# Expert weights in seven packed pieces: how a routed mixture kernel stores and loads its weight forms

## The chip, the cores and the metric

The kernel runs on one core of one Trainium2 chip. The metric is the device time of one execution in microseconds. Of the kernel before there are three runs with a median of 901.46 us. One further execution was recorded by the hardware profiler, and all views of the profile come from it. Engines: PE is TensorE (its weight loads are shown as PEld), DVE is VectorE, ACT is ScalarE, POOL is GpSimd, SP is SyncE, which here issues nearly all DMAs. L1030 means line 1030 of the kernel before.

## The reference

All data are float32. An attention with polynomial features gives `x` (4352 tokens, 128 features), and a mixture of eight experts works on it; each token goes through every expert, with the weights `P` of a Sinkhorn iteration:

```
q_p, k_p = phi(q), phi(k)                 # products of two sketches of 8 numbers: 64 features
num = q_p @ (k_p^T v);  den = q_p . sum(k_p) + 1e-6
x = (num / den)  as (4 * 1088 tokens, 4 heads * 32)
P = exp(x @ w_gate - max); 8 times: rows to sum 1, columns to sum 1, P *= N / E
for e in range(8):                        # w1[e]: 128 x 1024, w2[e]: 1024 x 128
    out += P[:, e] * (relu(x @ w1[e]) @ w2[e])
```

## The kernel before

**Stages.** Attention and routing come first. PE's spare time in them is filled with experts 0 and 1 on part of the tokens, without `P` (`steps()`, written out by `fill`). While the routing runs, the generator `second_forms()` prepares sums of the second weights in HBM. From about 193 us on `weighted()` does all that is left: tokens from 1344 on for experts 1 to 7, the earlier tokens for experts 2 to 7. Since `P` is positive, it is multiplied into `x` ahead of the first product. All engines of this stage run in the order in which the code is written (`manual_schedule`), SP with its queue of DMAs too: a DMA that waits holds all later DMAs of SP.

**Items and half steps.** `wgroups` lists ten groups of token columns (two blocks of 256 columns each in the first five groups, of 224 in the others), `witems` the 60 pairs of a group and an expert. Every second group goes through its experts backwards, so that two items in a row share an expert where a group ends. An item has two half steps (`todo`, s = 0 and 1), each for half of the 1024 hidden features. In the loop over t the generators `firsts(t)` (first products, relu and sums) and `seconds(t - 1)` (second products of the half step before) take turns, product by product.

**Seven products instead of eight.** Both matrix products are done on two by two blocks with seven products of blocks (Winograd's form of Strassen's method) in place of eight. That needs sums of the weight blocks, the forms, besides the blocks themselves. Of the first weights there are eight pieces in the tile `w1x` [128, 8, 256]: four raw blocks (0 to 3) and four sums (4 to 7, made by `sum_first`, L864, on POOL). `firsts` uses seven of them, in the order 0, 4, 5, 7, 6, 2, 3 (L1102 to L1134); raw block 1 is only an input of the sums. Of the second weights `seconds` uses three of the four raw blocks of the tile `w2` [128, 8, 128] and the four sums in the tile `ws` [128, 4, 4, 64]. The last group (`whole`) takes the plain eight products of the second weights, with raw blocks only.

**Where the forms come from.** In the first group (items 0 to 6) and at item 13 the first weights are loaded raw from the input (L857, four DMAs of 128 KB), summed on POOL, and written to a store in HBM (`store_first`, L872, 1 MB). These items are the set `fresh`. All later items load the finished 1 MB tile (L852). The sums of the second weights are built in HBM by `second_forms`: SP writes one half of a sum (`begin`), POOL adds the other half with accumulating DMAs (`add_first`, `add_second`, `add_third`, L905). An item then loads raw `w2` from the input (L861, 512 KB) and `ws` from the store (L862, 512 KB).

**When the weights are loaded.** All three tiles come from pools with two buffers. In the first half step of item i `prepare(i + 1, False)` (L1275) asks for the next item's first weights, in the second half step `prepare(i + 1, True)` (L1283) for its second weights. An item that shares its expert with the one before takes over its tiles.

**What else goes through SP and POOL.** Each item needs a row of `P` spread over all partitions (`load_weights`, L934, for item i + 3), the product of `x` and `P` on POOL (`weigh`, L942) with two DMAs that swap halves of its partitions (L945, for item i + 2), and differences of blocks of `x` (`sum_x`: L951 on POOL, L953 and L955 on DVE). `gate` (L1047) is a copy of one column on ACT that holds POOL's step back until ACT has come to that place. DVE adds PE's results to copies (L1034) and makes the sums of the hidden blocks (L1080 to L1085). At the end of a group its sums are added up (L1218), turned and stored.

Of the kernel before, what the change touches and what calls it, by code (L numbers as in the profile page):

```python
# [50 lines left out]
def kernel(  # L51
# [791 lines left out]
    def form_tiles():  # L843
        return (late[0].tile([P, 8, FORM], F32, tag="w1x", name="w1x"),
                wpool.tile([P, FO, DM], F32, tag="w2", name="w2"),
                wpool.tile([P, 4, FO // 2, H2], F32, tag="ws", name="ws"))

    def load_first(w, e, stored):


        if stored:
            nc.sync.dma_start(out=w[0], in_=form_stores[e][0])  # L852
            return
        for r in range(2):
            for k in range(2):
                rows = H2 * (r ^ k)
                nc.sync.dma_start(out=w[0][H2 * r:H2 * (r + 1), 2 * k:2 * k + 2],  # L857
                                  in_=moe_w1[e][rows:rows + H2].rearrange("p (i r n) -> p r i n", i=2, r=2)[:, r])

    def load_second(w, e):  # L860
        nc.sync.dma_start(out=w[1], in_=moe_w2[e].rearrange("(fo fi) d -> fi fo d", fi=P))  # L861
        nc.sync.dma_start(out=w[2], in_=form_stores[e][1])  # L862

    def sum_first(i):  # L864
        w1, g = forms[i][0], nc.gpsimd
        g.tensor_tensor(w1[:, 4], w1[:, 1], w1[:, 3], op=Alu.add)
        g.tensor_tensor(w1[:, 5], w1[:, 4], w1[:, 0], op=Alu.subtract)
        g.tensor_tensor(w1[:, 6], w1[:, 0], w1[:, 1], op=Alu.subtract)
        g.tensor_tensor(w1[:, 7], w1[:, 2], w1[:, 5], op=Alu.subtract)

    def store_first(i):
        nc.sync.dma_start(out=form_stores[witems[i][1]][0], in_=forms[i][0])  # L872

    def second_forms():
# [9 lines left out]
        for e in range(1, E):  # L884
            form_stores[e] = (dram.tile([P, 8, FORM], F32, name=f"w1x{e}"),
                              dram.tile([P, 4, FO // 2, H2], F32, name=f"ws{e}"))
# [9 lines left out]
        def begin(e):  # L896
            w, f = rooms[e], form_stores[e][1]
            pin(nc.scalar.mul(w[:, 0], w[:, 0], -1.0))
            pin(nc.sync.dma_start(out=f[:, 0].rearrange("p f d -> p (f d)"), in_=flat(w[:, 1, 0:4])))
            pin(nc.sync.dma_start(out=f[:, 1:3].rearrange("p m f d -> p m (f d)"),  # L900
                                  in_=flat(w[:, 0, 0:4]).unsqueeze(1).to_broadcast([P, 2, FO // 2 * H2])))
            pin(nc.sync.dma_start(out=flat(f[:, 3]), in_=flat(w[:, 0, 4:8])))

        def add(e, out, x):
            pin(nc.gpsimd.dma_start(out=flat(form_stores[e][1][:, out]), in_=flat(x), accum_op=Alu.add))  # L905

        def add_first(e):
            for m in (1, 2):
                add(e, m, rooms[e][:, 1, 0:4])

        def add_second(e):
            for m in (0, 1):
                add(e, m, rooms[e][:, 1, 4:8])

        def add_third(e):
            add(e, 3, form_stores[e][1][:, 1])
# [39 lines left out]

    def same(i):
        return 0 < i < len(witems) and witems[i - 1][1] == witems[i][1]

    def prepare(i, second):  # L960

        if i >= len(witems):
            return
        if same(i):
            forms[i] = forms[i - 1]
            return
        if not second:
            forms[i] = form_tiles()
        if second:
            load_second(forms[i], witems[i][1])  # L970
        else:
            load_first(forms[i], witems[i][1], i not in fresh)
# [24 lines left out]
    def weighted():  # L997
# [16 lines left out]
        def firsts(t):  # L1014
# [10 lines left out]
            def product(out, form, x, start, stop):  # L1025
                for r in range(2):
                    rows = slice(H2 * r, H2 * (r + 1))
                    for col in range(2):
                        o = P * s + H2 * col
                        nc.tensor.matmul(out[H2 * col:H2 * (col + 1), r], w1[rows, form, o:o + H2], xf[rows, x],  # L1030
                                         start=start, stop=stop, tile_position=(H2 * r, H2 * col), skip_group_check=True)

# [375 lines left out]
```

## Time and profile before

| what | value |
| --- | --- |
| three runs | 901.41, 901.46, 903.54 us; median 901.46 |
| the profiled execution | 902.27 us, of which 900.5 from the first to the last instruction (span) |
| mean granted TensorE clock | 0.998 |
| matmuls of the weighted stage | first at 193.0 us, 13489 of them to the end |
| DMA traffic, whole span | 189.90 MB |
| DMA share of the 16 engines, 193 us to the end | 0.69 |

How to read the rows: a group row gives the count of an instruction, its busy time and the mean time of one. A row of waits gives who waited for whom, the us in total, how often, and the longest. "issue" stands for time in which the engine waited for nothing that the profile shows. A windows row gives the stretch in us, its length, the busy time and count of each engine, the granted clock (1.00 is full speed), the share of the 16 DMA engines that was busy (it can come out a little above 1) and GB/s. In the rows of DMA queues q1 is the queue of SP's DMAs and q8 and q14 carry the engines' instructions; a q row gives packets, MB and the share of the engines.

### The profile page before, as it was taken

The page shows a single profiled execution, that of the slowest core. Times are in us where ns is not written, and L with a number is a line of the kernel's source. Part 1 is how long each engine was busy: PE and PEld are TensorE (multiplying, and loading weights), DVE is VectorE, ACT ScalarE, POOL GpSimd, SP SyncE. Part 2 cuts the span into 40 slices and gives each one's busy share as a digit, 9 for nine tenths or more (in the row PEclk, how much of TensorE's full clock was granted, in tenths as well). Part 3 has the DMA queues.
Part 4 walks back from the last instruction along what each step waited for, and adds up shares of the span by engine and source line. Part 5 has one row for each costly group of instructions (what it writes and reads, how often), then busy time and mean ns, then how long its engine had stood idle before and what let it go on. Part 6 is the DMA issues. An engine that isn't in the chain of part 4 may idle for free.

```text
span 900.5 us, 35855 instructions
## 1 busy us (share of the span) xinstructions
PE 888.7 (99%) x15372; PEld 647.6 (72%) x15372; DVE 762.6 (85%) x1325; ACT 546.4 (61%) x1089; POOL 271.0 (30%) x313
## 2 busy tenths in 40 slices
PE   9999999999999998999999999999999999999997
PEld 5777644557667775677777777677897799887896
DVE  7678789888898888888888888888898889889885
ACT  3455476646666664666666666666666666666664
POOL 3121148035551234223213322332232223223220
PEclk9999999999999999999999999999999999999999
DMA  8998599467886873687478658655974984875863
GB/s 240 298 282 243 111 196 201 79 177 230 249 247 189 282 236 110 198 266 230 146 222 246 227 149 241 220 186 153 295 254 106 276 268 132 291 224 187 261 198 90
DMA packets 150686, 189.90 MB, mean 211 GB/s; under 512 B 44512, under 2 KB 122416, under 8 KB 143616
## 3 DMA queue, kind: packets, MB, share of 16 engines
q1 hardware_dynamic: 142784, 177.52, 65.5%
q0 software_dynamic: 6640, 9.95, 5.8%
q8 instruction: 121, 1.98, 0.9%
q14 instruction: 37, 0.30, 0.1%
q10 hardware_dynamic: 1104, 0.15, 0.1%
HBM read 144.97 MB, written 24.16 MB: 188 GB/s over the span
## 4 chain that ended last, share of the span: by engine, by line
PE 95%; DVE 3%; issue 1%; ACT 1%; POOL 0%; DVEq 0%; POOLq 0%
PE pair L1030 38%; PE s L1164 38%; PE a L711 7%; PE s L772 7%; PE a L305 1%; PE a L118 1%; PE a L420 1%; DVE hb L726 1%; PE a L272 0%; DVE hb L1034 0%; PE s L334 0%; PE a L384 0%; DVE hb L1083 0%; PE a L454 0%; PE s L350 0%
## 5 line engine op out<-in xcount | busy, mean ns | idle before, releaser
L1030 PE MATMUL pair<-xf,w1x 64*64 64x256 f32 (+1 forms) x6736 | 513.2, 366 | 1.2 <-DVE hb L1034 1.1
L1030 PEld LDWEIGHTS pair<-xf,w1x 64*64 64x64 f32 x6736 | 269.0, 133 | 87.3 <-DVE hb L1034 7.0
L1034 DVE TENSOR_TENSOR hb<-pair,copies 128x512 f32<-128x512 f32 (+1 forms) x354 | 233.9, 662 | 74.5 <-ACT xf L1047 29.2
L1164 PE MATMUL s<-hb,ws 64*64 64x256 f32 (+1 forms) x3712 | 285.0, 366 | 2.5 <-DVE hb L1084 1.9
L1164 PE MATMUL s<-hb,w 64*64 64x256 f32 (+1 forms) x3040 | 229.6, 364 | 1.2 <-issue 1.2
L1037 ACT ACTIVATE hb<-hb 128x512 f32<-128x512 f32 (+1 forms) x240 | 145.7, 608 | 107.4 <-DVE hb L1034 102.1
L1164 PEld LDWEIGHTS s<-hb,ws 64*64 64x64 f32 x3712 | 153.6, 133 | 47.6 <-DVE hb L1084 2.7
L942 POOL TENSOR_TENSOR xf<-xT,pb 128x512 f32<-128x512 f32 (+1 forms) x60 | 73.4, 1224 | 278.7 <-ACT xf L1047 248.6
L1164 PEld LDWEIGHTS s<-hb,w 64*64 64x64 f32 x3040 | 124.7, 133 | 37.6 <-issue 2.8
L951 POOL TENSOR_TENSOR xf<-xf 128x512 f32<-128x512 f32 (+1 forms) x58 | 70.8, 1222 | 217.7 <-ACT xf L1047 139.0
L711 PE MATMUL a<-xT,w 128*64 128x416 f32 (+3 forms) x512 | 121.2, 466 | 0.0
L1037 ACT ACTIVATE hb<-pair 128x512 f32<-128x512 f32 (+1 forms) x126 | 72.5, 575 | 45.6 <-PE pair L1030 45.6
L713 ACT ACTIVATE hb<-a 128x416 f32<-128x416 f32 (+3 forms) x128 | 59.6, 468 | 65.5 <-PE a L711 53.8
L1080 DVE SCALAR_TENSOR_TENSOR hb<-hb 128x512 f32<-128x512 f32 (+1 forms) x116 | 77.9, 671 | 13.5 <-ACT hb L1037 1.7
L1112 ACT COPY copies<-pair 128x512 f32<-128x512 f32 (+1 forms) x118 | 66.5, 563 | 31.7 <-PE pair L1030 31.7
L1109 ACT COPY copies<-pair 128x512 f32<-128x512 f32 (+1 forms) x118 | 66.5, 563 | 30.7 <-PE pair L1030 30.7
L1103 ACT COPY copies<-pair 128x512 f32<-128x512 f32 (+1 forms) x118 | 66.6, 565 | 27.5 <-PE pair L1030 27.5
L1084 DVE SCALAR_TENSOR_TENSOR hb<-hb 128x512 f32<-128x512 f32 (+1 forms) x116 | 81.9, 706 | 0.0
L1083 DVE TENSOR_TENSOR hb<-hb 128x512 f32<-128x512 f32 (+1 forms) x116 | 78.1, 673 | 3.6 <-ACT hb L1037 0.5
L1085 DVE TENSOR_TENSOR hb<-hb 128x512 f32<-128x512 f32 (+1 forms) x116 | 79.4, 685 | 0.0
L726 DVE TENSOR_TENSOR hb<-hb 128x416 f32<-128x416 f32 (+7 forms) x84 | 59.7, 710 | 19.2 <-ACT hb L713 13.4
L772 PE MATMUL s<-hb,ws 128*64 128x416 f32 (+3 forms) x224 | 70.6, 475 | 0.5 <-DVE hb L726 0.4
(179 smaller groups left out, 677.6 us busy)
## 6 DMA issues: line engine op xcount, KB each, us to landing
w1x<-w1x SPq DMA_DIRECT2D x51, 1024.0 KB, 5.8
w<-in_moe_w_dram SPq DMA_DIRECT2D x56, 512.0 KB, 5.4
ws<-ws SPq DMA_DIRECT2D x52, 512.0 KB, 6.3
pb<-pT SPq DMA_DIRECT2D x35, 256.0 KB, 5.6
xf<-xf SPq DMA_DIRECT2D x70, 128.0 KB, 2.8
pb<-pT SPq DMA_DIRECT2D x25, 224.0 KB, 7.4
xf<-xf SPq DMA_DIRECT2D x50, 112.0 KB, 4.5
w1x<-in_moe_w_dram SPq DMA_DIRECT2D x32, 128.0 KB, 4.0
```

What stands on the lines that cost most here:

```text
L711: nc.tensor.matmul(ph[sl], loaded_w[j][0][:, P * f + H2 * s:P * f + H2 * (s + 1)], xT[:, at + lo:at + hi], start=True, stop=True, tile_pos ...
L772: nc.tensor.matmul(sums[g][i][H2 * s:H2 * (s + 1)], w, x, start=c == 1, stop=c == per, tile_position=(0, H2 * s))
L942: nc.gpsimd.tensor_tensor(xf[:, 0:2].rearrange("p b n -> p (b n)"), xT[:, lo:lo + 2 * n], weights.pop(i), op=Alu.mult)
L951: engine.tensor_tensor(xf[:, 4:6], xf[:, 1:4:2], xf[:, 0:2], op=Alu.subtract)
L1030: nc.tensor.matmul(out[H2 * col:H2 * (col + 1), r], w1[rows, form, o:o + H2], xf[rows, x], start=start, stop=stop, tile_position=(H2 * r, ...
L1034: nc.vector.tensor_tensor(flat(out, n), x, flat(y, n), op=Alu.add)
L1037: nc.scalar.activation(out=x, in_=y, func=Act.Relu)
L1080: nc.vector.scalar_tensor_tensor(ts[:, 0], h[:, 3], 0.0, h[:, 0], op0=Alu.max, op1=Alu.subtract)
L1083: nc.vector.tensor_tensor(ts[:, 2], h[:, 1], ts[:, 0], op=Alu.subtract)
L1084: nc.vector.scalar_tensor_tensor(ts[:, 1], h[:, 3], 0.0, h[:, 1], op0=Alu.max, op1=Alu.subtract)
L1085: nc.vector.tensor_tensor(ts[:, 3], h[:, 2], ts[:, 2], op=Alu.subtract)
L1164: yield lambda rho=rho, rows=rows, c=c: nc.tensor.matmul(acc[g][rho][q][H2 * half:H2 * (half + 1), n * place:n * (place + 1)], w[rows], fl ...
```

## The change

- The store of the first weights keeps seven pieces instead of eight, in the order of use (`PLACE`); raw block 1, which no product reads, stands last in the tile and isn't stored.
- The store of the second weights keeps the seven pieces that `seconds` uses: raw blocks 00 and 01, F3, F0, F2, F1, raw block 11. `begin` now also copies raw 00 and 01 from the input and raw 11 from its room; two of POOL's accumulating DMAs become one over F2 and F1.
- The buffers are taken once (`open_forms`): two of each tile, used in turn by item (`nth` counts changes of expert). The former tiles `w2` and `ws` together hold the seven pieces of the second weights.
- Loads are DMAs of up to two pieces (256 KB). They are issued in the second half step of item i, right behind the product that used the old content, for the item after next in that count (`next_of(i, 2)`): four in `firsts`, four in `seconds` (which runs one half step later).
- Items 0 and 1 get their second weights ahead of the loop and at t = 0, ahead of item 1's raw first weights. Raw loads for `fresh` items stay where they were.
- The last group's items load one raw block from the input, in F0's place, and leave out F2 and F1.

The core of the diff:

```diff
+    PLACE = {f: n for n, f in enumerate((0, 4, 5, 7, 6, 2, 3, 1))}
+    RAW00, RAW01, F3, F0, F2, F1, RAW11 = range(7)
+    nth = [sum(witems[j][1] != witems[j - 1][1] for j in range(1, i + 1)) for i in range(len(witems))]
...
+    def open_forms():
+        w1 = [late[0].tile([P, 8, FORM], F32, name=f"w1x{k}", bufs=1) for k in range(2)]
+        w2 = [wpool.tile([P, FO, DM], F32, tag="w2", name="w2").rearrange("p (m f) d -> p m (f d)", m=4)
+              for _ in range(2)]
+        ws = [wpool.tile([P, 4, FO // 2, H2], F32, tag="ws", name="ws").rearrange("p m f d -> p m (f d)")
+              for _ in range(2)]
+        for i in range(len(witems)):
+            forms[i] = [t[nth[i] % 2] for t in (w1, w2, ws)]
...
+    def next_of(i, ahead):
+
+        if i + 1 < len(witems) and nth[i + 1] == nth[i]:
+            return None
+        return next((j for j in range(i, len(witems)) if nth[j] == nth[i] + ahead), None)
...
+    def load_first(i, lo, hi):
+        nc.sync.dma_start(out=forms[i][0][:, lo:hi], in_=form_stores[witems[i][1]][0][:, lo:hi])
+
+    def load_second(i, part_):
+        e, (_, w2, ws) = witems[i][1], forms[i]
+        f = form_stores[e][1]
+        if part_ == 1 and witems[i][0] in whole:
+            nc.sync.dma_start(out=w2[:, F0].rearrange("p (f d) -> p f d", d=H2),
+                              in_=moe_w2[e].rearrange("(fo fi) d -> fi fo d", fi=P)[:, 0:FO // 2, H2:DM])
+        elif part_ < 2:
+            nc.sync.dma_start(out=w2[:, 2 * part_:2 * part_ + 2], in_=f[:, 2 * part_:2 * part_ + 2])
+        elif part_ == 3 or witems[i][0] not in whole:
+            lo, hi = ((0, 2), (2, 3))[part_ - 2]
+            nc.sync.dma_start(out=ws[:, lo:hi], in_=f[:, 4 + lo:4 + hi])
...
     def store_first(i):
-        nc.sync.dma_start(out=form_stores[witems[i][1]][0], in_=forms[i][0])
+        nc.sync.dma_start(out=form_stores[witems[i][1]][0], in_=forms[i][0][:, 0:7])
...
             pin(nc.scalar.mul(w[:, 0], w[:, 0], -1.0))
-            pin(nc.sync.dma_start(out=f[:, 0].rearrange("p f d -> p (f d)"), in_=flat(w[:, 1, 0:4])))
-            pin(nc.sync.dma_start(out=f[:, 1:3].rearrange("p m f d -> p m (f d)"),
+            pin(nc.sync.dma_start(out=f[:, RAW00:RAW01 + 1].rearrange("p m (f d) -> p (m f) d", d=H2),
+                                  in_=moe_w2[e].rearrange("(fo fi) d -> fi fo d", fi=P)[:, :, 0:H2]))
+            pin(nc.sync.dma_start(out=f[:, F0:RAW11 + 1:RAW11 - F0],
+                                  in_=w[:, 1].rearrange("p (m f) d -> p m (f d)", m=2)))
+            pin(nc.sync.dma_start(out=f[:, F2:F1 + 1],
                                   in_=flat(w[:, 0, 0:4]).unsqueeze(1).to_broadcast([P, 2, FO // 2 * H2])))
...
+            coming = next_of(i, 2) if s else None
+
+            def fetch(lo, hi):
+                if coming is not None and coming not in fresh:
+                    load_first(coming, lo, hi)
...
             product(pc, 4, 4, True, True)
+            fetch(0, 2)
...
             product(pc, 7, 3, False, True)
+            fetch(2, 4)
...
             product(pc, 2, 2, True, True)
+            fetch(4, 6)
...
             product(pa, 3, 7, False, True)
+            fetch(6, 7)
...
+                    if r == 1:
+                        fetch(m)
                     yield
             both(into(0, raw(1, 1, 0), ts[:, 3], 0, 1, 1), into(1, raw(1, 1, 1), ts[:, 3], 1, 1, 1))
+            fetch(3)
...
+                if t == 0:
+                    for part_ in range(4):
+                        load_second(1, part_)
                 if s == 0:
-                    prepare(i + 1, False)
+                    if i + 1 in fresh:
+                        load_raw(i + 1)
...
-                else:
-                    prepare(i + 1, True)
...
-        prepare(0, False)
-        prepare(0, True)
+        open_forms()
+        load_raw(0)
+        for part_ in range(4):
+            load_second(0, part_)
```

More of the change, by code (lines that the diff above doesn't have):

```diff
@@ L841, with form_of, load_raw @@
     FORM = FO * H2 // 2
[L843 to L853, printed above, removed]
+    PLACE = {f: n for n, f in enumerate((0, 4, 5, 7, 6, 2, 3, 1))}
[9 more added lines that the diff above has]
+            forms[i] = [t[nth[i] % 2] for t in (w1, w2, ws)]
+    def form_of(i, m):
+        _, w2, ws = forms[i]
+        return w2[:, m] if m < 4 else ws[:, m - 4]
+    def next_of(i, ahead):
+        if i + 1 < len(witems) and nth[i + 1] == nth[i]:
+            return None
+        return next((j for j in range(i, len(witems)) if nth[j] == nth[i] + ahead), None)
+    def load_raw(i):
+        w, e = forms[i], witems[i][1]
         for r in range(2):
@@ L884, in second_forms @@
         for e in range(1, E):
[L885 to L886 removed]
+            form_stores[e] = (dram.tile([P, 7, FORM], F32, name=f"w1x{e}"),
+                              dram.tile([P, 7, FO // 2 * H2], F32, name=f"w2x{e}"))
         def load(e):
@@ L1146, in seconds, with fetch @@
             lo, n, es = wgroups[g]
-            _, w2, ws = forms[i]
             h, ts = rooms(t)
+            coming = next_of(i, 2) if s else None
+            def fetch(part_):
+                if coming is not None:
+                    load_second(coming, part_)
             if g not in acc:
```

57 lines of the change are left out of this document (22 added, 35 removed).

## The prediction, made before the changed kernel was run

> **What bounds the kernel now.** I read the page's busy shares first, then the waits, then the stage after 193 us in windows. The page's first part, and from its third part the queue that carries TensorE's instructions (packets, MB, share):
>
> ```profile
> PE 888.7 (99%) x15372; PEld 647.6 (72%) x15372; DVE 762.6 (85%) x1325; ACT 546.4 (61%) x1089; POOL 271.0 (30%) x313
> ...
> q8 instruction: 121, 1.98, 0.9%
> ```
>
> TensorE is busy for 888.7 of 900.5 us, so no edit that leaves its matmuls alone can win more than the 11.8 us of its idle time and what a lowered clock costs. This change leaves them alone. The question is therefore which holes PE has and who makes them. The waits of the weight loads after 193 us (us in total, times, longest) name them:
>
> ```profile
> PEld pair L1030 <- DVE hb L1034: 7.0, 17, 1.3
> PEld s L1164 <- issue: 4.3, 9, 0.9
> ```
>
> The other releasers there are DVE and ACT lines. None is a DMA: **PE never waits for a weight transfer today.** The second row is the odd one. "issue" means that PE waited for nothing that the profile shows, in the middle of a run of equal matmuls. Where that happens, four-microsecond windows show it beside steady ones (columns: PE, PEld, DVE, ACT, POOL busy with their counts, granted clock, DMA share, GB/s):
>
> ```profile
> 346.00:350.00 4.00, 2.12 (x36) 0.96 (x28) 4.00 (x4) 0.58 (x2) 2.73 (x3) 1.00 0.81 282
> 350.00:354.00 4.00, 3.13 (x33) 1.93 (x36) 3.14 (x6) 1.45 (x3) 0.00 (x0) 0.57 0.00 0
> 644.00:648.00 4.00, 3.54 (x74) 2.77 (x68) 2.56 (x5) 1.88 (x4) 1.81 (x2) 1.00 0.96 358
> 650.00:700.00 50.00, 50.00 (x1058) 43.55 (x1050) 44.94 (x85) 33.04 (x68) 15.49 (x17) 1.00 0.64 192
> 660.00:664.00 4.00, 4.00 (x92) 3.94 (x86) 3.76 (x7) 2.48 (x6) 1.76 (x2) 1.00 0.85 274
> 716.00:720.00 4.00, 3.46 (x68) 2.41 (x62) 3.77 (x8) 2.66 (x5) 1.07 (x2) 1.00 1.10 246
> 724.00:728.00 4.00, 3.81 (x81) 3.54 (x77) 3.38 (x7) 2.33 (x5) 0.80 (x1) 1.00 0.93 239
> 845.00:849.00 4.00, 3.77 (x79) 3.01 (x75) 3.70 (x8) 2.29 (x5) 0.65 (x1) 1.00 0.63 152
> 852.00:856.00 4.00, 3.51 (x71) 3.02 (x70) 3.42 (x7) 2.10 (x5) 0.00 (x0) 1.00 0.95 303
> ```
>
> A steady window of the 224-column groups holds 92 matmuls (660 us). Five windows hold 74, 68, 81, 79 and 71, together 87 short. At 50.00 / 1058 = 47.3 ns a matmul that is **4.1 us of PE**. The 346 us hole, with its lowered clock, is a different one; I come back to it.
>
> My reading of the five: PE's own instructions come late. 1.98 MB in 121 packets are 16.4 KB each, and PE's 2 x 15372 instructions over 121 are 254 to a packet. A half step of the 224-column groups is 112 matmuls and 112 weight loads, 112 x 47.3 ns = 5.3 us, so PE eats a packet in 254 / 224 x 5.3 = 6.0 us. Now the DMA view of the stretch 707.5 to 717.25 us ahead of the hole at 716 to 720 us, and of an equally long one, 660.5 to 670.2 us, without a hole:
>
> ```profile
> q1 hardware_dynamic: 1577, 2.58, 91.4%
> issues: line engine op xcount, KB each, median us to landing
> w1x<-w1x SPq DMA_DIRECT2D x1, 1024.0 KB
> w<-in_moe_w_dram SPq DMA_DIRECT2D x1, 512.0 KB, 8.8
> ```
>
> ```profile
> q1 hardware_dynamic: 1471, 2.43, 76.1%
> q8 instruction: 1, 0.02, 0.8%
> ```
>
> In the first there is no q8 row at all: for 9.75 us not one instruction packet was served, with the data queue at 91.4% of all engines, and then PE stands. In the second, at 76.1%, one came through. So instruction packets sit behind long bursts of data, and when one is late by about 4 us PE runs dry. A sentence on the Trainium skill: "Runtime: NRT & Kernel Launch", section "Instruction fetch mechanics", has the same 16 KiB blocks of 256 instructions and says that crossing to the next is mostly hidden; by that the five holes would have another cause and the change would win nothing (the second rival).
>
> **The change part by part.** (1) *Bytes and bursts of the weighted stage.* The loads of items with 224 columns, in the DMA view of 650 to 700 us (KB each, median us to landing):
>
> ```profile
> w1x<-w1x SPq DMA_DIRECT2D x4, 1024.0 KB, 8.1
> w<-in_moe_w_dram SPq DMA_DIRECT2D x3, 512.0 KB, 4.7
> ws<-ws SPq DMA_DIRECT2D x3, 512.0 KB, 5.2
> pb<-pT SPq DMA_DIRECT2D x5, 224.0 KB, 7.1
> xf<-xf SPq DMA_DIRECT2D x8, 112.0 KB, 2.4
> ```
>
> Now 1024 + 512 + 512 + 224 + 2 x 112 = 2496 KB per item, 2048 KB of them in two blocks of 1 MB. After: two times seven pieces of 128 KB, 896 + 896, so 2240 KB, 10% less, in eight issues of at most 256 KB. A piece is issued only when PE is done with the old one, so the eight are spread over about two half steps (10.6 us). The 2.58 MB burst above took 9.75 us at 264 GB/s; one piece at that rate is 1 us. A packet then finds a backlog of one or two pieces, some 2 us, where lateness of about 4 us is needed for a hole. I take **all five holes as gone, -4.1 us**; bounds 0 (bursts only move) and -5 (the -4.1 and the rest of that 4.3 us row).
>
> (2) *When the pieces must be there.* Each is fetched for the item after next. The first of w1's is issued after the second product of a half step and needed one item and most of a half step later, over 14 us; w2's pieces likewise. The worst landing in the rows above is 8.8 us. No wait on PE, cost 0. If it failed, PE would stand for the lateness.
>
> (3) *SP.* Three issues per item become eight, about 0.4 us each, and wait for PE. What stands behind them on SP's queue, from the waits of that queue:
>
> ```profile
> SPq L945 <- POOL xf L942: 235.8, 59, 12.5
> SPq L852 <- PE pair L1030: 77.4, 23, 4.5
> SPq L576 <- DVE qT L574: 30.8, 1, 30.8
> ```
>
> SP already spends its time waiting, and today's w1 load (L852) waits for PE too. The new waits stand in the order in which PE works, so the swaps of x (L945), the rows of P and the stores behind them are held to a point that PE has passed anyway; the swaps are used an item later. Cost 0.
>
> (4) *Start of the stage.* At t = 0 the four pieces of item 1's second weights come ahead of item 1's raw w1, and they wait until PE has left the old w2 and ws. Rows of SP, PE and POOL there (start, us), and ahead of them the page's row for raw w1:
>
> ```profile
> w1x<-in_moe_w_dram SPq DMA_DIRECT2D x32, 128.0 KB, 4.0
> ...
> 187.84 2.51 SPq L857 DMA_DIRECT2D w1x<-in_moe_w_dram  x4
> ...
> 191.53 1.56 PE L772 MATMUL s<-hb,ws 128*64 128x416 f32 x6
> ...
> 196.38 1.08 POOL L866 TENSOR_TENSOR w1x<-w1x 128x256 f32<-128x256 f32 x1
> ...
> 199.93 1.17 POOL L869 TENSOR_TENSOR w1x<-w1x 128x256 f32<-128x256 f32 x1
> ...
> 205.98 0.64 PE L1030 MATMUL pair<-xf,w1x 64*64 64x256 f32 x8
> ```
>
> The raw w1 is issued at 187.84 to 190.35 now. After: pieces until about 194, raw w1 194 to 196.5, landing 4.0 us later (first row), 200.5, instead of in time for 196.38. POOL's four sums take 201.10 - 196.38 = 4.7 us and end at 205.2; the last is needed at 205.98. It just fits: 0. Bounds: -1 (DVE's steps before 200 us are free of POOL's company) and +4 (landing after 8.8 us).
>
> (5) *Preparing the forms, before 193 us.* Per expert, the raw 256 KB of w2 copied within HBM and 128 KB of a fourth quarter are added, 7 x 384 KB = 2.75 MB, and one POOL issue of five goes. Those windows:
>
> ```profile
> 150.00:160.00 10.00, 10.00 (x70) 5.03 (x68) 9.02 (x19) 7.99 (x17) 8.27 (x10) 1.00 1.10 144
> 160.00:170.00 10.00, 9.88 (x66) 5.12 (x63) 9.60 (x18) 3.81 (x8) 0.84 (x2) 1.00 0.25 37
> ```
>
> The engines are full until 160 us and a quarter busy after. At 144 GB/s the added bytes need 19 us; they spill past 160, where SP waits for DVE anyway (L576 above, 30.8 us, until 173.3). PE works on without them. Cost 0; bounds -1 (POOL's issues) and +3 (spill past 175 into the first rows of P).
>
> (6) *The hole at 346 us* (start, us):
>
> ```profile
> 345.13 1.11 DVE L1083 TENSOR_TENSOR hb<-hb 128x512 f32<-128x512 f32 x1
> ...
> 346.17 3.12 DVE L1084 SCALAR_TENSOR_TENSOR hb<-hb 128x512 f32<-128x512 f32 x1
> ```
>
> Two DVE steps of one size take 1.11 and 3.12 us while POOL, busy for 2.73 of these 4 us (first window above), works off what has gathered behind item 13's four sums. PE idles 4.00 - 2.12 + 4.00 - 3.13 = 2.75 us and works 3.13 us at clock 0.57, another 1.3: about 4.1 us. The change keeps those sums and their gates. I leave it in: 0, bounds -4.1 (a shifted DMA moves POOL's start) and +4.1 (a second such meeting).
>
> **Sum.** -4.1 + 0 + 0 + 0 + 0 + 0. The profiled execution took 902.27 us, so 898.2; the median shown is 901.46, 0.8 lower, and against it **897.4 us** (-0.45%). The 0.8 us also bounds what profiling itself may add to the holes.
>
> **Rivals.** *B: the hole at 346 us goes as well.* Speaks for it: it hangs on one meeting of DVE and POOL. Against: their order of work is unchanged. 897.4 - 4.1 = 893.3.
>
> *C: the transfers are hidden anyway and the five holes stay or move.* For it: 76.1% and 91.4% are not far apart, and the rule on hidden fetching. Against: the missing q8 row just ahead of a hole. 901.5, within 1.5.
>
> *D: the pieces bunch, and the holes multiply: slower.* SP waits up to 12.5 us at L945; if pieces pile up behind it they leave together, and 2240 KB an item is still two thirds of a busy queue. A hole is worth 4.1 / 5 = 0.8 us. At every other one of the 25 items with 224 columns that is 10 us, less 4.1 now: +5.9, **907**. It decides from a backlog of some 6 us, one packet's time, so SP would have to be held for most of an item. Against: the 12.5 us are SP arriving early, POOL's product itself follows PE's step by a few us. Beside it: "DMA: Bandwidth & Descriptors", section "Bandwidth", of the Trainium skill advises batches of at least 1 MiB, which speaks for D and against this change. Here the rows do not go by size (512 KB in 5.2 us, 224 KB in 7.1): the queue ahead decides, so I give it little weight.
>
> *E: the change makes PE wait for each piece*, should a write to a part of a fixed buffer be ordered against reads of other parts. Four waits of about 5 us per item would cost hundreds of us. Against it, products of DVE on thirds of one tile and PE's reads of another third:
>
> ```profile
> 34.38 1.83 DVE L411 TENSOR_TENSOR ph<-ph,rb 128x768 f32<-128x768 f32 x2 [4.73 <-DMA rb<-qb]
> 35.47 0.90 PE L420 MATMUL a<-kvs,ph 128*64 128x66 f32 x24
> ```
>
> PE starts on the first third at 35.47, while DVE writes the second until 36.21: parts are told apart.
>
> **How the numbers follow.** The forecast 0.45, B 0.13, C 0.24, D 0.16, E 0.02. About 0.3%, 2.7 us, is what a measurement here can tell from no change: below 898.8 faster, above 904.2 slower. Faster: 0.39 of the forecast's 0.45 and B, 0.52. Same: the remaining 0.06 and C, 0.30. Slower: D and E, 0.18. The forecast alone spans 895 to 900. The range takes in B to its lower side and C with the start's +4 less part of the gain: 892 to 903.5; D and E, and a little below, are left out.
>
> **What would show it.** Right: "PEld s L1164 <- issue" falls from 4.3 us to about 1, windows of 4 us in the 224-column groups hold 92 throughout, the DMA share has no stretch of 10 us above 0.9, 10% fewer MB in the stage. Step 4: the raw w1 lands near 200.5 and no PE idle time between 203 and 207 us. Step 5: PE's first L1030 still at 193.0. Wrong: "issue" rows that stay or grow (C, D), "PE <- DMA" rows (step 2, E), DVE steps over 2 us at new places (step 6).

## The result, and the profile after

The changed kernel takes **896.9 us** (median of 13 runs, 895.77 to 899.35) where the kernel before, run beside it on the same chip, takes 901.41 us (13 runs, 899.79 to 907.09): a ratio of 0.9951, 95% interval 0.9936 to 0.9967, so faster by 4.5 us, half a percent and clear of the noise. Its profiled execution took 895.77 us, with a span of 894.0; before it was 902.27 and 900.5.

The profile page of the changed kernel: busy shares, the queue that carries TensorE's instructions (packets, MB, share), and the commonest loads (count, KB each, median us to landing):

```profile
PE 884.1 (99%) x15372; PEld 630.6 (71%) x15372; DVE 762.9 (85%) x1325; ACT 546.6 (61%) x1089; POOL 270.2 (30%) x306
...
q8 instruction: 122, 2.00, 0.9%
...
w1x<-w1x SPq DMA_DIRECT2D x132, 256.0 KB, 3.8
w<-w2x SPq DMA_DIRECT2D x102, 256.0 KB, 3.6
```

The matmuls are as many as before, and the idle time of PE fell from 11.8 to 9.9 us. The 1 MB blocks that took 5.8 us over the whole page, and 8.1 us in the stage shown before, are pieces that take under 4. The page's total of DMA traffic is 178.44 MB, 11.46 less. The waits of the weight loads from 193 us on (us in total, times, longest):

```profile
PEld pair L1044 <- DVE hb L1054: 8.7, 17, 2.9
PEld pair L1044 <- issue: 0.4, 1, 0.4
```

L1044 are the first products now, L1194 the second ones. The row "PEld s ... <- issue", 4.3 us before, is no longer there, and no DMA is named as a releaser. (The row of before was not all holes of the 224-column groups: four of its nine waits, 3.3 us, lie there. One of 0.27 us is at 200.6 us, and four of 0.18 us are at 351 to 354 us, where the clock was lowered. Of the five windows counted in the prediction, the one at 724 us has its wait, 0.40 us, under the name of DVE's L1084. The 0.4 us left in the changed kernel are a pause of 0.35 us at 203.7 us; the kernel before has one of 0.32 us at the same step, in all three of its profiles.) Windows of four microseconds where the holes of the 224-column groups had been (each about 2 to 6 us earlier now, as the kernel is ahead):

```profile
642.00:646.00 4.00, 4.00 (x92) 3.23 (x88) 3.41 (x8) 2.61 (x6) 1.84 (x2) 1.00 0.58 155
714.00:718.00 4.00, 4.00 (x92) 3.19 (x88) 3.54 (x9) 2.44 (x6) 0.71 (x1) 1.00 0.74 223
722.00:726.00 4.00, 4.00 (x91) 3.20 (x84) 3.65 (x8) 2.64 (x6) 1.77 (x2) 1.00 0.84 260
840.00:844.00 4.00, 4.00 (x92) 3.24 (x88) 3.72 (x8) 2.93 (x6) 0.57 (x1) 1.00 0.78 230
846.00:850.00 4.00, 4.00 (x92) 3.22 (x85) 3.50 (x8) 2.91 (x6) 0.00 (x0) 1.00 0.85 269
```

They hold 91 or 92 matmuls, the full number, where those of before held 68 to 81. The DMA view of a stretch of 9.75 us at the place where the view of before had no row of q8:

```profile
q1 hardware_dynamic: 1735, 2.76, 91.1%
q8 instruction: 2, 0.03, 1.3%
```

The data queue is about as busy as in the stretch of before (91.1% here, 91.4% there), and two instruction packets come through. So the share of busy DMA engines, on which the prediction partly relied as a sign, doesn't tell the two apart. The missing row of q8 doesn't either: the view counts a packet where it starts. In the kernel before one packet started at 707.43 us, just ahead of the stretch, and took until 710.04; the next came at 717.30. Starts as far apart as 9.2 us also occur in the changed kernel's first profile, which has no such hole.

The place at 346 us, in DVE's and POOL's rows of the changed kernel (start, us) and in two windows:

```profile
344.74 1.11 DVE L1103 TENSOR_TENSOR hb<-hb 128x512 f32<-128x512 f32 x1
345.77 1.21 DVE L1104 SCALAR_TENSOR_TENSOR hb<-hb 128x512 f32<-128x512 f32 x1
346.91 1.75 DVE L1105 TENSOR_TENSOR hb<-hb 128x512 f32<-128x512 f32 x1
...
341.74 0.74 POOL L893 TENSOR_TENSOR w1x<-w1x 128x256 f32<-128x256 f32 x1
```

```profile
346.00:350.00 4.00, 1.71 (x32) 0.83 (x24) 4.00 (x4) 0.40 (x2) 3.17 (x3) 1.00 0.76 262
350.00:354.00 4.00, 3.82 (x72) 2.76 (x76) 3.71 (x8) 2.92 (x5) 0.00 (x0) 1.00 0.32 98
```

The longest step of DVE here is 1.75 us instead of 3.12, and the clock of the next window stays at 1.00 (0.57 before). PE idles 2.47 us in the two windows, 2.75 before. The hole is still there, but smaller. The start of the stage (start, us):

```profile
192.57 4.34 PE L1044 MATMUL pair<-xf,w1x 64*64 64x256 f32 x72
...
191.34 0.80 SPq L885 DMA_DIRECT2D w<-w2x  x2
192.67 0.80 SPq L888 DMA_DIRECT2D ws<-w2x  x2
193.52 2.52 SPq L872 DMA_DIRECT2D w1x<-in_moe_w_dram  x4
...
199.42 0.89 POOL L893 TENSOR_TENSOR w1x<-w1x 128x256 f32<-128x256 f32 x1 [3.44 <-DMA w1x<-in_moe_w_dram]
...
202.27 0.91 POOL L896 TENSOR_TENSOR w1x<-w1x 128x256 f32<-128x256 f32 x1
```

POOL does wait for the raw weights behind the new pieces, and its sums end at 203.2 us, in time. And SP's waits:

```profile
SPq L976 <- POOL xf L973: 143.9, 59, 7.2
SPq L876 <- PE pair L1044: 75.5, 116, 4.0
SPq L885 <- PE s L1194: 36.2, 46, 1.5
```

SP waits for the pieces (L876, L885) and less at the swaps of x (235.8 us before, 143.9 now).

**A measure for the holes.** ACT makes one copy in nearly every half step (L1109 before, L1130 after; 118 copies for 120 half steps), so a hole shows as a longer distance between two of them. "Other holes" below is the sum of what such distances have above the shortest of the two kernels' five profiles at the same half step, where it is over 0.1 us, from the twelfth half step on and without the one at 346 us; that one is given against its neighbours (6.05 us). "Spread" is the standard deviation of the time between two packets of q8 from 640 us on, whose mean is about 6 us.

**The single packets.** The trace has the start and end of each packet of q8. The last column counts the idle time of PE's weight loads on "issue" from 212 us on that ends 1.0 to 1.8 us after the end of such a packet. Left out are the stretches behind the hole at 346 us in which the trace has the granted clock at 0.5; there PE shows an even row of pauses of 0.16 to 0.18 us on "issue". Of the 64 waits that remain in the 14 profiles, 60 end in that interval, 1.22 to 1.71 us behind a packet. With a packet every 6 us, chance would put about one in eight there. So PE stands until its next packet has come: that these holes are late instructions is shown, and not only argued from what else is missing.

| profile | span us | hole at 346 us | other holes | spread of packets | stops behind a packet, us (times) |
| --- | --- | --- | --- | --- | --- |
| before | 900.5 | 4.63 | 4.66 (7 places) | 1.60 | 3.29 (4) |
| before, again | 895.3 | 3.29 | 0.79 (3) | 1.44 | 0.26 (1) |
| before, third | 898.8 | 4.97 | 2.36 (6) | 1.41 | 1.26 (2) |
| after | 894.0 | 2.69 | 0 | 1.14 | 0 |
| after, again | 894.3 | 2.70 | 0.57 (1) | 1.26 | 0.42 (1) |
| run 1, packed, whole blocks | 898.5 | 6.33 | 0.80 (2) | 1.33 | 0.50 (1) |
| run 5, pieces, old bytes | 899.1 | 4.38 | 3.09 (7) | 1.54 | 2.71 (5) |
| run 2, old load cut | 903.7 | 4.88 | 7.45 (12) | 1.52 | 6.02 (9) |
| run 6, long packets | 901.5 | 3.19 | 6.68 (7) | 1.49 | 3.44 (3) |
| run 4, spread copies | 910.4 | 6.27 | 12.36 (15) | 1.74 | 3.97 (5) |
| run 3, burst copies | 930.3 | 3.21 | 28.04 (29) | 1.58 | 18.37 (22) |
| run 7, before, lighter | 899.8 | 1.51 | 7.49 (6) | 1.71 | 6.92 (5) |
| run 8, after, lighter | 893.9 | 1.27 | 0.69 (2) | 1.23 | 0.42 (1) |
| run 9, early sums | 893.2 | 0.00 | 0.31 (1) | 1.25 | 0.17 (1) |

The kernels that load 2240 KB an item (after, run 1, runs 8 and 9) have 0 to 0.50 us of such stops in five profiles, those that load 2496 KB (before, runs 2, 5, 6 and 7) 0.26 to 6.92 us in seven, spread or not.

### The profile page after: what moved, and what is told of

It reads as the page before. It is cut to its first block, busy times and chain, and to the rows that moved or that the text cites. A ratio compares the mean times of both kernels' runs of the same rounds, so it can differ in the third digit from the quotient of the medians.

```text
span 894.0 us, 36522 instructions
## 1 busy us (share of the span) xinstructions
PE 884.1 (99%) x15372; PEld 630.6 (71%) x15372; DVE 762.9 (85%) x1325; ACT 546.6 (61%) x1089; POOL 270.2 (30%) x306
## 2 busy tenths in 40 slices
DMA packets 146628, 178.44 MB, mean 200 GB/s; under 512 B 56448, under 2 KB 94288, under 8 KB 146080
## 4 chain that ended last, share of the span: by engine, by line
PE 94%; DVE 5%; ACT 1%; issue 1%; POOL 0%; DVEq 0%; ACTq 0%; POOLq 0%
PE pair L1044 39%; PE s L1194 38%; PE a L711 6%; PE s L772 6%; DVE hb L726 2%; PE a L305 1%; PE a L420 1%; PE a L118 1%; PE a L272 0%; PE s L334 0%; PE a L384 0%; DVE rs L554 0%; DVE cs L560 0%; DVE p L557 0%; DVE hb L1054 0%
## 5 line engine op out<-in xcount | busy, mean ns | idle before, releaser
L1044 PE MATMUL pair<-xf,w1x 64*64 64x256 f32 (+1 forms) x6736 | 496.3, 365 | 2.6 <-DVE hb L1054 2.5
L1044 PEld LDWEIGHTS pair<-xf,w1x 64*64 64x64 f32 x6736 | 255.2, 133 | 96.3 <-DVE hb L1054 8.7
L1194 PE MATMUL s<-hb,w 64*64 64x256 f32 (+1 forms) x3904 | 290.0, 364 | 0.0
L1194 PE MATMUL s<-hb,ws 64*64 64x256 f32 (+1 forms) x2848 | 213.6, 365 | 0.0
L1194 PEld LDWEIGHTS s<-hb,w 64*64 64x64 f32 x3904 | 151.9, 133 | 50.3
L1194 PEld LDWEIGHTS s<-hb,ws 64*64 64x64 f32 x2848 | 111.2, 133 | 36.1 <-DVE hb L1104 0.2
L1100 DVE SCALAR_TENSOR_TENSOR hb<-hb 128x512 f32<-128x512 f32 (+1 forms) x116 | 78.0, 672 | 14.0 <-ACT hb L1057 1.8
L1130 ACT COPY copies<-pair 128x512 f32<-128x512 f32 (+1 forms) x118 | 66.5, 564 | 29.6 <-PE pair L1044 29.6
L1104 DVE SCALAR_TENSOR_TENSOR hb<-hb 128x512 f32<-128x512 f32 (+1 forms) x116 | 79.4, 685 | 0.0
```

What stands on the lines that cost most here:

```text
L1044: nc.tensor.matmul(out[H2 * col:H2 * (col + 1), r], w1[rows, PLACE[form], o:o + H2], xf[rows, x], start=start, stop=stop, tile_position=(H ...
L1100: nc.vector.scalar_tensor_tensor(ts[:, 0], h[:, 3], 0.0, h[:, 0], op0=Alu.max, op1=Alu.subtract)
L1104: nc.vector.scalar_tensor_tensor(ts[:, 1], h[:, 3], 0.0, h[:, 1], op0=Alu.max, op1=Alu.subtract)
L1194: yield lambda rho=rho, rows=rows, c=c: nc.tensor.matmul(acc[g][rho][q][H2 * half:H2 * (half + 1), n * place:n * (place + 1)], w[rows], fl ...
```

## The experiments

**The theory:** PE's instruction packets wait behind a backlog of data; fewer bytes and pieces spread over the item shorten it, and that is the gain. **Rivals:** the gain comes from fewer bytes alone, or from the cut alone, or from longer packets of the packed store; or it comes from the meeting of DVE and POOL at 346 us; or the holes are chance and the profiles shown were a bad and a good one.

The two parts of the change apart come first, then the disputed mechanism by itself, then the hole at 346 us, then the repeats. "Before" is always the kernel before, run beside it on the same chip.

**1. The packed store, loaded in whole blocks at the old places** (from the changed kernel):

```diff
-            coming = next_of(i, 2) if s else None
+            coming = None
...
+                coming = next_of(i - 1, 2) if i else None
+                if coming is not None and s == 0 and coming not in fresh:
+                    load_first(coming, 0, 7)
...
+                    nc.sync.dma_start(out=forms[coming][1], in_=f[:, 0:4])
+                    nc.sync.dma_start(out=forms[coming][2][:, 0:3], in_=f[:, 4:7])
```

> The changed kernel's packing (seven pieces, 10% fewer bytes per item), but loaded in two blocks of 896 KB at the places where the kernel before loads its blocks of 1 MB. Theory (an instruction packet of PE comes late behind a long backlog of data, and PE stands): part of the holes comes back, since the bursts are only an eighth smaller; 1 to 3 us of idle time on issue in PE's weight loads after 193 us, 898 to 900 us. Rival (the bytes alone made the gain): no idle time on issue, 897. Rival (the gain came from loading further ahead): all of it comes back, 901.

Measured: 899.19 us, before 901.13; ratio 0.9974 (0.9957 to 0.9991). Its waits from 193 us on:

```profile
PEld s L1194 <- issue: 1.4, 8, 0.2
PEld pair L1044 <- issue: 1.4, 6, 0.5
```

The time lies in the range expected by the theory, 1.9 us or two fifths of the gain, but the rows don't say what the theory wants. Of these 14 waits 13 are the even pauses of the halved clock, from 351 to 357 us, such as

```profile
351.44 0.25 PEld L1194 LDWEIGHTS s<-hb,ws 64*64 64x64 f32 x4 [0.18 <-issue]
351.87 0.25 PEld L1194 LDWEIGHTS s<-hb,ws 64*64 64x64 f32 x4 [0.18 <-issue]
```

and one alone, 0.50 us at 725 us, ends behind a packet. So with fewer bytes in whole blocks the late packets are nearly gone. Most of what this profile has above that of after, 3.6 of 4.5 us, is the hole at 346 us.

**2. The old 1 MB load cut into four, at its old place** (from the kernel before):

```diff
-            nc.sync.dma_start(out=w[0], in_=form_stores[e][0])
+            for m in range(0, 8, 2):
+                nc.sync.dma_start(out=w[0][:, m:m + 2], in_=form_stores[e][0][:, m:m + 2])
```

> The kernel before with its 1 MB load of w1x cut into four loads of 256 KB, issued one behind the other at the old place: same bytes and same burst, packets of 2 KB in place of 8 KB. Theory (length of the backlog): the holes stay, about 4 us on issue, 901.4 within 1. Rival (large packets hold up the instruction packets): they go, 897.

Measured: 904.0 us, before 901.13; ratio 1.0034 (1.0017 to 1.0052). The theory expected 901.4 within 1. The cut alone, with all four issued at once, is no gain but a small loss, with 7.45 us of holes in its profile. A smaller DMA by itself doesn't help.

**3 and 4. Extra copies within HBM into unused places, the same number of bytes an item, in bursts and spread** (from the changed kernel; the copies feed nothing). The burst is 2 MB at the start of every second item:

```diff
+                if s == 0 and i % 2 == 0:
+                    for m in range(4):
+                        nc.sync.dma_start(out=unused[m], in_=moe_w1[m])
```

Spread, four pieces of 256 KB in every item:

```diff
+            nc.sync.dma_start(out=unused[2 * s], in_=moe_w1[s][:, 0:F // 2])
...
+            nc.sync.dma_start(out=unused[2 * s + 1], in_=moe_w1[s][:, F // 2:F])
```

> The changed kernel, with 2 MB copied within HBM at the start of every second item, in one burst, into tensors that nobody reads. No engine waits for these copies. Theory: the backlog is 5 to 8 us each time, instruction packets come late again, and holes of about 0.8 us return in the groups with 224 columns, at up to 12 places, fewer in the groups with 256 columns, where a packet lasts longer: 900 to 908 us, idle time on issue of 3 us or more. Rival (the holes of the kernel before had nothing to do with the queues of the DMAs): 897, no issue rows.

> The changed kernel with the same number of unused bytes as the burst kernel on average (1 MB per item), but as four copies of 256 KB at four places of every item. Theory: the bytes do no harm when they are spread; idle time on issue under 1 us, 896 to 899 us. Rival (what counts is the sum of bytes, not the burst): as slow as the burst kernel.

Measured: the burst 933.21 us, ratio 1.036 (1.0327 to 1.0392); spread 911.28 us, ratio 1.0107 (1.0074 to 1.0141); before 901.13 for both. The waits of the burst's weight loads, from 193 us on:

```profile
PEld s L1195 <- issue: 16.2, 20, 2.1
PEld pair L1045 <- issue: 8.6, 12, 2.3
```

and of the spread one:

```profile
PEld pair L1045 <- DVE hb L1055: 12.4, 21, 3.6
PEld s L1197 <- issue: 5.4, 13, 1.2
PEld pair L1045 <- issue: 2.5, 9, 0.7
PEld s L1197 <- DMA w<-w2x: 1.5, 2, 1.2
```

This is the clearest run on the mechanism. No product reads the copies, and still PE stands for 24.8 us on "issue" in the burst; 18.4 us of that, in 22 stops, end 1.2 to 1.6 us behind an instruction packet. With the copies spread it is 4.0 us in 5 stops. Both kernels keep the DMA engines busy at 0.90 from 193 to 880 us, so at these bytes the burst makes the difference. The times went far beyond what was expected, though: 900 to 908 us for the burst, 896 to 899 for the spread copies, which were to do no harm. With the same bytes the burst costs 36 us over the changed kernel and the spread pieces 14. Most of the 14, and part of the 36, is no late instruction but data that comes late (the DMA row) and engines that are held, DVE in the spread kernel, POOL and ACT in the burst.

**5. The other half of the change: pieces spread as in the changed kernel, with the old number of bytes.** The eighth piece of w1 is stored and loaded again, and one piece of w2 is loaded twice, 2496 KB an item:

```diff
+            if part_ == 3:
+                nc.sync.dma_start(out=ws[:, 3:4], in_=f[:, 6:7])
...
-        nc.sync.dma_start(out=form_stores[witems[i][1]][0], in_=forms[i][0][:, 0:7])
+        nc.sync.dma_start(out=form_stores[witems[i][1]][0], in_=forms[i][0])
...
-            fetch(6, 7)
+            fetch(6, 8)
```

> The changed kernel with the bytes of the kernel before: the eighth piece of the first weights is stored and loaded too, and one piece of the second weights is loaded twice (into a part of the tile that nobody reads), so 2496 KB per item, still in pieces as PE leaves the old ones. With the earlier run of the packing in whole blocks this fills a table of bytes and bursts. If the spreading alone is enough: no holes on issue, 897. If the bytes did most of it, as that run suggests: 1 to 4 us of holes come back, 898 to 901.

Measured: 899.03 us, before 900.84; ratio 0.9981 (0.9964 to 0.9999). Its waits:

```profile
PEld pair L1046 <- issue: 2.5, 8, 0.8
PEld s L1196 <- issue: 2.1, 6, 1.1
```

By the medians the spreading alone gives about 1.8 us, the bytes alone (run 1) 1.9, both 4.5; the intervals are too wide to say more than that each has a part. By the stops the parts differ. Here 2.71 us of them end behind a packet, in the one profile no less than before: at the size of this change the profiles point to the bytes as what makes late packets rare. That the spreading helps against them is shown only where the queue is fuller (runs 3 and 4).

**6. The kernel before with raw w2 read in long packets** (a copy of the raw weights in HBM, laid out as the tile is):

```diff
-        nc.sync.dma_start(out=w[1], in_=moe_w2[e].rearrange("(fo fi) d -> fi fo d", fi=P))
+        nc.sync.dma_start(out=w[1], in_=form_stores[e][2])
```

> The kernel before, but the raw second weights are copied once into HBM in the order of the tile, so that their 512 KB arrive in packets of 4 KB rather than of 512 bytes; bytes, blocks and places as before. If the slow short packets made the backlog long (in the trace a stretch of them moves about 260 KB a us, one of long packets 390): most of the 4.3 us on issue goes, 897 to 899. If it is the sum of bytes: the holes stay, 901.

Measured: 903.24 us, before 900.84; ratio 1.0028 (1.0009 to 1.0048). In 650 to 700 us there are 4287 packets instead of 7624, the queue is 60.5% busy instead of 62.4%, and the holes stay (6.68 us). So the packets' size is not the cause, and a slightly emptier queue doesn't help either. Why the kernel is 2.4 us slower is not known.

**7 and 8. The meeting at 346 us made lighter, before and after:** at item 13 DVE takes the difference that POOL took, and POOL is given no step of the group's end in that half step. The same edit on both kernels:

```diff
-            engine = nc.vector if i == 1 else nc.gpsimd
+            engine = nc.vector if i in (1, 13) else nc.gpsimd
...
-                if g == 0:
+                if g == 0 or i + 1 in fresh:
```

> The kernel before, with less on POOL around item 13: the difference of blocks of x for item 13 (L951) is made on DVE, and POOL takes no leftover work in item 12. Theory (the hole at 346 us is a meeting of DVE's steps with a run of POOL's products behind the four sums of item 13; apart from the instruction holes): the hole shrinks from 4.6 us to under 1, the instruction holes of about 4.3 us on issue stay: 897 to 898. Rival (that hole also came from late instructions or late data): no change, 901.4.

> The same edit on the changed kernel. Theory: its hole there of 2.7 us shrinks to under 1, and the half steps elsewhere stay: 894.5 to 895.5. Rival: DVE, which gets one more step of 0.7 us, is now the late one at that place, and the hole stays at 2 to 3 us: 897.

Measured: before with it 900.7 us, ratio 0.9991 (0.9973 to 1.0009); after with it 897.01 us, ratio 0.9952 (0.993 to 0.9975); before 901.36 for both. The hole shrinks to 1.51 and 1.27 us in their profiles, not under 1 as expected, and neither kernel gets measurably faster by it (897 to 898 and 894.5 to 895.5 were expected). In the profile of before with it the late packets were the most of all seven profiles with the old bytes:

```profile
PEld s L1164 <- issue: 6.7, 5, 3.0
```

With the same edit in both, the kernels still differ by 3.7 us. So the change's gain isn't only this meeting.

**9. The hole at 346 us taken away:** item 13 isn't fresh, its sums are made and stored ahead of the stage (from the changed kernel):

```diff
-    fresh = {*range(len(wgroups[0][2])), witems.index((1, 1))}
+    fresh = {*range(len(wgroups[0][2]))}
...
+        sum_first(0)
+        store_first(0)
```

> The changed kernel, with expert 1's four sums made and stored by POOL just ahead of the stage, where it idles, so that item 13 loads finished pieces like the items around it and the four sums at 342 us are gone. If the hole there (2.7 us in the changed kernel) comes from these sums: it goes whole, and up to 1 us is lost at 186 to 191 us, where the sums now run beside DVE: 894.5 to 896. If it is an accident of phase that goes elsewhere: 897.

Measured: 896.39 us, ratio 0.995 (0.9929 to 0.9971), before 900.84. The windows and, in the chain that leads into the stage, PE's rows:

```profile
346.00:350.00 4.00, 4.00 (x80) 2.85 (x76) 3.63 (x7) 2.40 (x6) 1.53 (x2) 1.00 0.72 217
350.00:354.00 4.00, 4.00 (x84) 2.79 (x80) 3.77 (x7) 2.81 (x5) 0.44 (x1) 1.00 0.72 216
```

```profile
191.13 0.56 PE L772 MATMUL s<-hb,ws 128*64 128x416 f32 x1 [0.74 <-DVE hb L726]
...
194.06 4.34 PE L1044 MATMUL pair<-xf,w1x 64*64 64x256 f32 x72
```

PE is full in both windows: the sums at that place were the cause. But the stage begins at 194.06 instead of 192.57 us, and the chain names 0.74 us of waiting for DVE, beside whose work the same sums now stand. What is won at 346 us (2.7) is mostly given back (1.5 there and 0.4 in the first half step). That all of the 1.5 us are the sums' doing isn't shown: the unchanged kernel before began its stage at 194.26 us in its third profile. Its median is the lowest of all runs, but not by more than the interval.

**10, 11 and 12. The two kernels again, unchanged**, one execution of each:

> The kernel before once more, for a second profile: how much of the holes is the same from one execution to the next. If they are laid down by the program: the same five places within 0.3 us each. If they hang on chance in the memory: other places, a like sum.

> The kernel before, unchanged: a third profile of it. The first had 4.3 us of such idle time at five places (span 900.5), the second 0.5 us at two (span 895.3). Theory (the backlog makes holes likely, and where they fall is chance): 1 to 5 us, at other places than in the first, span 896 to 901. Rival (the holes are laid down by the program, the second profile was an exception): the five places of the first again.

> The kernel after, unchanged: a second profile of it. Theory (the data backlog behind which PE's instruction packets come late is what the change takes away): again no idle time of the weight loads put down to issue in the first products after 193 us, or at most 0.5 us of it, and a span of 893 to 895.5 us. Rival (holes come and go by chance in both kernels, and the first profile of after was a lucky one): 1.5 to 4 us of such idle time, and a span of 896 to 898.

Measured: the kernel before 897.12 and 900.63 us, the changed one 896.05. The waits of before, third profile:

```profile
PEld s L1164 <- DVE hb L1084: 2.4, 1, 2.4
PEld s L1164 <- issue: 2.2, 7, 0.7
PEld pair L1030 <- issue: 1.5, 5, 0.7
```

and its rows at 346 us, with POOL's first sum:

```profile
346.57 3.12 DVE L1084 SCALAR_TENSOR_TENSOR hb<-hb 128x512 f32<-128x512 f32 x1
...
342.55 0.74 POOL L866 TENSOR_TENSOR w1x<-w1x 128x256 f32<-128x256 f32 x1 [0.24 <-DMA w1x<-in_moe_w_dram]
```

The changed kernel's second profile, with a span of 894.3 us as the theory expected (its wait on "issue" is a late packet, at 731 us):

```profile
PEld pair L1044 <- issue: 0.4, 1, 0.4
```

On the question where the holes fall, each side was half right. Places come again (the half step at about 644 us in all three profiles of before, those at about 720 and 849 in two), but the hole at 644 us is 0.96, 0.41 or 0.69 us, and at the others one profile has none. So some places are likelier than others, and the size, down to nothing, is set by the execution. What the change moves is steadier than the holes: the spread of the packets is 1.41 to 1.60 us in three profiles of before, 1.14 and 1.26 in two of after.

The windows behind the hole at 346 us in the second profile of before and in run 5:

```profile
350.00:354.00 4.00, 2.98 (x56) 2.17 (x60) 3.71 (x7) 2.35 (x4) 0.08 (x1) 1.00 0.01 3
350.00:354.00 4.00, 3.24 (x41) 2.13 (x45) 3.71 (x8) 1.82 (x3) 0.00 (x0) 0.74 0.36 79
```

The first, with 3.06 us of idle PE from 346 us on, kept its clock at 1.00; the second, with 2.46 us, did not.

## Why the prediction came out right, step by step

The time was 896.9 us where 897.4 was forecast. The total is right, and two of its terms were wrong in opposite directions: that they nearly cancel is luck.

**Step 1, bytes and bursts: right in kind, too large.** The mechanism is the one named: PE's stops end 1.22 to 1.71 us behind an instruction packet, and runs 3 and 4 make them with data that nothing waits for. The size of 4.1 us came from a single profile, which was the worst of three: other holes of 4.66, 0.79 and 2.36 us, 2.6 in the mean, against 0 and 0.57 after. So the term is about **-2.3**, not -4.1. The prediction gave the gain to the shorter bursts and the fewer bytes together; of the two the table speaks for the bytes, and for the bursts nothing is shown at the size of this change. The sign that I named, no stretch of 10 us above 0.9, was wrong: the stretch is still there (91.1%). And "not one instruction packet was served" read too much into a stretch that began 0.07 us after a packet's start. Why the same share starves PE in one kernel and not in the other stays open. That pieces stand in the queue for 3.8 us and not 8.1 doesn't explain it: the cut loads of run 2 landed in 4.0 us in the same view of 650 to 700 us, and its profile has 6.0 us of stops.

By the Trainium skill, "Runtime: NRT & Kernel Launch", section "Instruction fetch mechanics", the crossing to the next block is mostly hidden. The changed kernel agrees (0 and 0.42 us of stops behind a packet in two profiles), the one before less (0.26 to 3.29), the burst not at all (18.4).

**Step 2, the pieces in time: right.** No row of PE names a DMA in either profile of after. **Step 3, SP: right.** Its waits moved to the pieces, and no row of PE names a transfer that stands behind them.

**Step 4, the start: right.** The raw weights were issued from 193.5 to 196.0 us (194 to 196.5 forecast), POOL started at 199.4 (200.5) and ended at 203.2 (205.2), with no loss of PE. **Step 5, the forms' preparation: right.** The stage begins at 192.57 us instead of 193.02, but in runs 5 and 8, which prepare the forms in the same way, at 192.99, so the 0.45 us aren't shown to come from it.

**Step 6, the hole at 346 us: wrong.** It was left in at 0. It shrank from 4.63, 3.29 and 4.97 us (mean 4.3) to 2.69 and 2.70: **-1.6**. Only 0.4 of that is PE's idle time from 346 to 354 us (2.75, 3.06 and 2.82, then 2.47 twice). The rest is the clock, granted at 0.57 and 0.67 in the window behind the hole in the first and third profile of before, at 1.00 in the second and in both of after. That this part belongs to the change isn't shown: run 5 has the idle time of after, and yet a clock of 0.74 and a hole of 4.38 us.

The 0.4 us go with POOL's start. Where its first sum follows POOL's product at once (after twice, run 5), DVE's longest step is 1.75 us and PE idles 2.46 to 2.47 us. Where it waits 0.18 to 0.31 us (before, its third profile, run 1), the step is 3.11 to 3.12 us and PE idles 2.75 to 2.88. Where it waits 0.45 to 0.73 us (the second profile of before, runs 2, 4 and 6), it is 2.43 to 2.44 us and 2.93 to 3.11. The row names the raw weights, a row of P or ACT for it. Every kernel that loads at the old place has this wait, run 1 with fewer bytes too, so here the spreading seems to be what counts; that was not tested alone. The bound of -4.1 covered it, the reason ("their order of work is unchanged") missed that the order can stay while the distance moves.

The sum by the spans: before 898.2 in the mean of three, after 894.15 of two, 4.05 apart. Of that 2.3 are other holes, 1.6 the one at 346 us. The rest cancels nearly: the stage starts 0.9 us earlier in the mean (192.57 us twice, against 193.02, 193.00 and 194.26), its first eleven half steps take 0.5 us more, and the tail is 0.3 us longer (12.56 and 12.51 us behind the last copy, 12.23 to 12.26 before).

**The rivals.** B (the hole at 346 us goes as well) happened in part, 1.6 of 4.1 us, most of it through the clock. C (the holes stay) is excluded by the interval. D (bunched pieces) didn't happen, but its mechanism is real: run 3 is what it looks like. There too stands the advice of the Trainium skill, "DMA: Bandwidth & Descriptors", section "Bandwidth", to batch at least 1 MiB: at equal bytes, cutting the 1 MB load into four at its place took 0.34% longer (run 2), which agrees, and pieces issued as their buffers come free took 0.19% less (run 5), which doesn't. E didn't happen.

## What to carry to other kernels

Where PE stands in the middle of equal matmuls with "issue" as the only releaser, look at the single packets that bring its instructions: where the stop ends a fixed time behind one (here 1.2 to 1.7 us), data that is early enough for its readers has still delayed them. The remedy that these runs point to is fewer bytes, and with a queue that is 0.90 busy, loads that don't come in bursts; merely smaller DMAs are none. Take more than one profile before a hole of a microsecond gets a price; here one program gave 0.8, 2.4 and 4.7 us. And where two engines meet at a hot spot, the cost can move by some tenths of a microsecond although nobody changed the order of work, and by more than one with the clock that is granted behind it.

## What the hardware did that I hadn't expected

- Stops behind an instruction packet differ from execution to execution of one program: 0.26 to 3.29 us in three profiles, with spans of 895.3 to 900.5. Whether they also make the wider scatter of the kernel before (899.79 to 907.09 us, 895.77 to 899.35 after) wasn't tested run by run.
- The instruction queue moves 2.00 MB of 178, 0.9% of the DMA engines' time, and with copies that feed nothing PE lost 18.4 us waiting for it.
- One DVE step on 128x512 takes 0.69 us at most places, 1.1 to 1.2 us beside POOL's sums, and at the one place near 347 us 1.75, 2.43 or 3.12 us, with the same value whenever POOL's sums begin equally late. What sets these values is open.
- The clock behind that place was granted at 0.52 to 0.83 in six of ten profiles and at 1.00 in four, and the length of PE's standstill doesn't tell which: 1.00 after 2.47, 2.97 and 3.06 us, 0.74 after 2.46.
